# The block behind a rarely taken branch, laid ahead of the branch's arm instead of behind it

## The chip, the cores and the metric

The kernel runs on one core of one Trainium2 chip. The metric is the device time of one execution in microseconds (us). The core has five engines, each with an instruction sequence of its own: PE (matrix products), DVE and ACT (vector and scalar work), POOL (here above all the issue of transfers) and SP (transfers). They wait for each other through semaphores.

## What is computed

Attention within a band of 32 positions to each side, in 8 batches of 8 heads with 576 positions of 64 values, followed by a mixture of 8 experts of which each token takes one:

```python
def _attn_ref(q, k, v):
    scores = scale * np.matmul(q, k.transpose(0, 1, 3, 2))
    mask = np.abs(pos[:, None] - pos[None, :]) <= window
    scores = np.where(mask, scores, -1000000000.0)
    ...
    return np.matmul(attn, v).astype(np.float32)

def _moe_ref(x, modality_id, w_gate, modality_bias, w1, w2):
    logits = x @ w_gate + modality_bias[modality_id]
    e_idx = np.argmax(logits, axis=1)
    ...
    for e in range(E):
        mask = e_idx == e
        h = np.maximum(x[mask] @ w1[e], 0.0)
        out[mask] = gate_w[mask, None] * (h @ w2[e])
```

There are 4608 tokens of 512 values; `w1` is 512 x 1024 and `w2` 1024 x 512 for each expert.

## The kernel before, in words

The program has two ways to the result. The **main part** is a fast way that rests on assumptions about the data: that only one expert is in use for each of the two modalities, that the sorted tokens of one modality fill about half of the list, that the sums of the softmax are in a normal range. It is written out by hand: the string `ORDER` lists its steps, and a loop calls the function of each step in that order, so every engine gets its instructions in the order of the string. Each batch's heads go through scores (`SA`, `SB`), exponentials (`sa`, `sb`), the band's mask (`M`), the product with the values (`V`) and the division by the sums (`v`). `X` sorts a block's tokens by modality, `pa` and `pb` append them to the two ends of `XT`. The expert's two products follow in tiles of 256 tokens (`U` at line 916, `u` at 931 and 933, `D` at 942), `y` scales the rows (952 and 954), and `O` (961) writes them to their places in the output with a scatter that POOL issues. Tile 18, the last, is a small one for the tokens where the two modalities meet.

The steps `c0` to `c16` check the assumptions along the way and count what breaks them; `c17` (line 1028) loads that count, `Ct["flag"]`, into a register of each of the five engines. In `ORDER` `c17` stands between the last scaling and the last two scatters:

```
... D18.0.0:2 y17.0/v O17.1/p D18.0.1 y18.0/a c17 O17.0/p O18.0/p
```

The **general arm**, `general()`, is a slow way that holds for any data. It stands under `tc.If(Ct["flag"] > 0, ...)` at line 1211 and computes everything anew, in loops over heads, batches and experts. With the inputs that are timed the count is zero, and the arm doesn't run.

The branch is compiled into three blocks for each engine besides the main part. The *arm* is `general()` with its loops. The *block behind the branch* is what runs in the arm's place: each engine waits for its own work and counts its semaphores up to where the arm would leave them. On POOL that is a row of waits for the eight software queues, thus for all scatters, and one instruction that adds to their semaphores (ISA in the order, INC_SWDGE_SEM in the profile). The profile gives this block line 1211, like the branch itself. The *end block* (line 1239) follows in both cases: SP checks all semaphores, the engines meet in a barrier, which POOL collects, POOL clears the semaphores, and they meet once more.

Before the change, these blocks lie in memory as main part, arm, block behind the branch, end block. The main part ends with a compare-and-branch on every engine. With a count above zero it falls through into the arm; with zero it jumps over the arm to the block behind the branch, which runs on into the end block.

Of the kernel before, what the change touches and what calls it, by code (L numbers as in the profile page):

```python
# [94 lines left out]
def kernel(  # L95
# [98 lines left out]
    Ct = {}  # L194
# [1013 lines left out]
            nc.sync.dma_start(ov[bass.ds(i, 1)].rearrange("a (t p) d -> p (a t) d", p=TB), acc)  # L1208

    tail = const.tile([P, 1], FP32)  # L1210
    with tc.If(Ct["flag"] > 0, preferred_fallthrough_block=True):
        for _ in range(1):
            nc.gpsimd.memset(tail[:], 0.0)
        general()
# [29 lines left out]
```

## Time and profile before

| | |
|---|---|
| time, median of 3 runs | 209.22 us (208.91 to 209.65) |
| the profiled execution's own time | 209.1 us |
| its span, first to last instruction | 207.5 us |
| granted TensorE clock, mean | 0.996 |
| PE, matrix products | 194.9 us busy, 94% of the span |
| DVE | 149.9 us, 72% |
| ACT | 133.0 us, 64% |
| POOL | 98.9 us, 48% |
| fetches of instructions, queues q8 and q14 | 22 packets of 0.36 MB, 12 packets of 0.10 MB |

How to read the rows: engines' names are as above; PEld is PE's loading of weights, and a q behind a name (POOLq) marks an instruction of the engine's sequencer, which waits, branches or drains while the engine itself may be idle or busy with earlier work. Such instructions are not in the busy times. L1211 is line 1211 of the kernel. Starts are in us from the start of the span.

### The profile page before, as it was taken

How to read it: one execution, taken by the hardware profiler on the slowest of the kernel's cores; microseconds unless marked ns; L12 is line 12 of the kernel's file. 1: busy time of each engine (PE TensorE's matmuls, PEld its weight loads, DVE VectorE, ACT ScalarE, POOL GpSimd, SP SyncE). 2: the span in 40 equal slices, each digit the busy share in tenths (PEclk: the TensorE clock that was granted, in tenths of full speed). 3: DMA queues.
4: the chain of work that ended last, by engine and by line, in shares of the span. 5: the costliest groups of instructions: out<-in, count | busy, mean ns of one | idle time of the engine just before them, and what ended most of it. 6: DMA issues, size and time to landing. Idle time of an engine off the chain costs nothing. (4 is left out here: it accounts for less than half of the span.)

```text
span 207.5 us, 6240 instructions
## 1 busy us (share of the span) xinstructions
PE 194.9 (94%) x2585; PEld 139.8 (67%) x2585; DVE 149.9 (72%) x293; ACT 133.0 (64%) x226; POOL 98.9 (48%) x143
## 2 busy tenths in 40 slices
PE   7689789999999999999999999999999999999980
PEld 5568569867766588559766885687578669765630
DVE  3888999999899788779799988975378442803210
ACT  3484697669794987776588878579653547060620
POOL 7987695686051979288102830660321011331351
PEclk9999999999999999999999999999999999999998
DMA  4999999999999999989992890239121831221141
GB/s 67 202 174 185 211 209 193 212 193 212 200 186 234 169 211 213 206 115 206 186 171 68 97 175 0 83 128 113 51 102 53 332 128 54 103 101 51 54 158 57
DMA packets 47629, 30.41 MB, mean 147 GB/s; under 512 B 38851, under 2 KB 38891, under 8 KB 47339
## 3 DMA queue, kind: packets, MB, share of 16 engines
q0 software_dynamic: 46576, 27.79, 84.2%
q1 hardware_dynamic: 1019, 2.16, 3.0%
q8 instruction: 22, 0.36, 0.7%
q14 instruction: 12, 0.10, 0.1%
HBM read 36.76 MB, written 9.70 MB: 224 GB/s over the span
## 5 line engine op out<-in xcount | busy, mean ns | idle before, releaser
L961 POOL DMA_INDIRECT out_dram<-ys,ids x37 | 40.6, 1098 | 87.2 <-ACT ys L952 33.8
L916 PE MATMUL banks<-XT,w_sb 128*128 128x256 bf16 x576 | 71.4, 273 | 0.3 <-DVE xt L758 0.3
L942 PE MATMUL banks<-w_sb,hT 128*128 128x512 bf16 x288 | 69.8, 379 | 0.0
L916 PEld LDWEIGHTS <-w_sb 128*128 128x128 bf16 x576 | 53.8, 98 | 10.9 <-issue 1.3
L695 ACT ACTIVATE pt<-banks 128x1536 bf16<-128x1536 f32 x32 | 46.4, 1453 | 14.0 <-PE banks L687 9.5
L933 ACT ACTIVATE hT<-banks 128x512 bf16<-128x512 f32 x57 | 33.0, 600 | 30.0 <-PE banks L916 27.5
L942 PEld LDWEIGHTS <-hT 128*128 128x128 bf16 x296 | 26.7, 98 | 25.6 <-issue 0.6
L655 DVE STREAM_TRANSPOSE qk<-qk 128x576 int32<-128x576 int32 x32 | 38.5, 1244 | 1.8 <-DMA qk<-in_q_dram 1.1
L712 DVE TENSOR_TENSOR pt<-pt,mask 128x1920 bf16<-128x1920 bf16 x28 | 32.1, 1169 | 3.5 <-ACT pt L695 3.4
L758 DVE TENSOR_TENSOR xt<-banks,recs 128x640 bf16<-128x640 f32 x32 | 26.4, 824 | 1.2
L729 PEld LDWEIGHTS <-pt 128*128 128x128 bf16 x576 | 21.2, 97 | 3.6 <-issue 0.4
L729 PE MATMUL banks<-vt,pt 128*128 128x65 bf16 x576 | 22.7, 193 | 0.4 <-DVE pt L712 0.2
L931 DVE TENSOR_SCALAR hT<-banks 128x512 bf16<-128x512 f32 x17 | 11.5, 685 | 15.9 <-PE banks L916 15.9
L952 ACT ACTIVATE ys<-banks,Gt 128x512 f32<-128x512 f32 x20 | 13.7, 691 | 12.9 <-PE banks L942 12.1
L798 ACT CAST XT<-banks 128x352 f32 (+3 forms) x40 | 18.0, 449 | 5.7 <-PE banks L778 4.9
L687 PE MATMUL banks<-qk 32*128 32x192 bf16 (+1 forms) x640 | 18.8, 239 | 2.5 <-DVE oh_ab L613 1.6
L231 POOL DMA_DIRECT2D vt<-in_v_dram x16 | 20.5, 1285 | 0.2 <-issue 0.2
L954 DVE TENSOR_SCALAR ys<-banks,Gt 128x512 f32<-128x512 f32 x17 | 12.7, 744 | 10.3 <-PE banks L942 4.7
L812 ACT CAST XT<-banks 128x352 f32 (+2 forms) x39 | 17.6, 452 | 1.9 <-PE banks L778 1.3
L687 PEld LDWEIGHTS <-qk 32*128 32x128 bf16 x640 | 12.3, 93 | 9.6 <-issue 6.8
L970 PE MATMUL banks<-zero_b 128*128 128x256 bf16 x88 | 13.1, 297 | 1.8 <-POOL zero_b L320 1.3
L778 PEld LDWEIGHTS <-xt 128*128 128x128 bf16 x160 | 10.5, 98 | 4.9 <-issue 0.8
(157 smaller groups left out, 146.3 us busy)
## 6 DMA issues: line engine op xcount, KB each, us to landing
vt<-in_v_dram POOLq DMA_DIRECT2D x16, 288.0 KB
w_sb<-in_moe_w_dram POOLq DMA_DIRECT2D x4, 1024.0 KB
qk<-in_q_dram POOLq DMA_DIRECT2D x7, 576.0 KB
qk<-in_k_dram POOLq DMA_DIRECT2D x7, 576.0 KB
wx<-w_sb SPq DMA_DIRECT2D x2, 1024.0 KB, 6.2
out_dram<-ys,ids POOLq DMA_INDIRECT x37
qk<-in_k_dram POOLq DMA_DIRECT2D x2, 288.0 KB
qk<-in_q_dram POOLq DMA_DIRECT2D x2, 288.0 KB
```

The costliest lines, as they stand in the source:

```text
L231: nc.gpsimd.dma_start(v_t[b % NV][:, n_ * i:n_ * i + n_, 0:D], v[b].rearrange("h s d -> (h s) d").rearrange("(n p) d -> p n d", p=P)[:, n_ ...
L655: nc.vector.transpose(qk_t[b % 2][:, g, at:at + S].rearrange("p (t r) -> p r t", r=R), Ct["l", b][:, u, g].bitcast(I32).rearrange("p (r j) ...
L687: nc.tensor.matmul(st[:, h, WIN * i_:WIN * i_ + w_], qk[32 * h:32 * h + 32, c_, QK + k0:QK + k0 + P], qk[32 * h:32 * h + 32, c_, q0:q0 + w ...
L695: nc.scalar.activation(pt[:, :, 2 * part:2 * part + 2, 0:WIN], st[:, :, 0:2 * WIN].rearrange("p h (j c) -> p h j c", c=WIN), ACT.Exp, scal ...
L712: nc.vector.tensor_tensor(out=p_ap, in0=p_ap, in1=mask[:], op=ALU.mult)
L729: nc.tensor.matmul(o_ap, pt[:, c1:c1 + P], vt[:, g0 + j, 0:D + 1], start=(m == 0 and i_ == 0), stop=(i_ == len(mine) - 1), skip_group_chec ...
L758: nc.vector.tensor_tensor(out=o_ap, in0=o_v[:, :, :, 0:D], in1=rec.unsqueeze(3).to_broadcast([P, 2, NM, D]), op=ALU.mult)
L798: ins = nc.scalar.copy(XT[:, :, bass.ds(r_, w_)], Ct["X", b, m][:, :, 0:w_])
L916: ins = nc.tensor.matmul(ph[:, u_, :], w1[:, f0:f0 + 2 * P - 1:2], rhs, start=(kd == 0), stop=(kd == n_kd - 1))
L933: nc.scalar.activation(o_ap, i_ap, ACT.Relu)
L942: nc.tensor.matmul(Ct["D", t_, s_], Ct["h", t_][:, kf, P * s_:P * s_ + P], w2, start=(kf == 0), stop=(kf == n_kf - 1))
L961: ins = nc.gpsimd.indirect_dma_start(out=out, out_offset=bass.IndirectOffsetOnAxis(ap=ids[:, u_:u_ + 1], axis=0), in_=Ct["y", t_, s_][:], ...
```

## The change

One argument of the branch is turned round:

```diff
-    with tc.If(Ct["flag"] > 0, preferred_fallthrough_block=True):
+    with tc.If(Ct["flag"] > 0, preferred_fallthrough_block=False):
         for _ in range(1):
             nc.gpsimd.memset(tail[:], 0.0)
         general()
```

After it the blocks lie as main part, block behind the branch, arm, end block. The compare-and-branch falls through into the block behind the branch when the count is zero, and jumps to the arm when it is not. At the end of the block behind the branch stands an unconditional branch over the arm to the end block. The instructions are the same in kind and number on every engine, and everything ahead of the compare-and-branch stands where it stood.

On POOL, at the end of the main part: the last scatters, the branch, and what follows it in memory (the queues' semaphores are DMASW0 to DMASW7; `tail` is the first tile that the arm writes).

```order
 L961 DMA out_dram<-ys,ids 4608x512 [waits DMASW2_49,Activation_49]
 L1211 COMPARE_AND_BRANCH
+L1211 ISA [waits Pool_49,DMASW4_49,DMASW5_49,DMASW3_49,DMASW6_49,DMASW2_49,DMASW7_49,DMASW1_49,DMASW0_49]
+L1211 UNCONDITIONAL_BRANCH
 L1213 MEMSET tail 128x1
 L1079 MEMSET XT 96x960 [waits PE_49]
```

The block behind the branch, with its waits for all eight queues, now follows the compare-and-branch. On POOL at the other end of the arm, whose last loop is at line 1154, and at the start of the end block (line 1239):

```order
 L1154 COMPARE_AND_BRANCH
 L1154 UNCONDITIONAL_BRANCH
-L1211 ISA
-L1211 UNCONDITIONAL_BRANCH
 L1239 ISA
```

There the two rows are gone, so that the arm runs on into the end block. Between the compare-and-branch and the old place of the block lie 58 rows on POOL, 59 on DVE, 21 on ACT and 40 on SP. On PE it is the same move, here at the end of the main part, behind the load of the count; the arm there has 422 rows, so that the jump over it is the longest:

```order
 L1028 TENSOR_LOAD fl_i
 L1211 COMPARE_AND_BRANCH
+L1211 UNCONDITIONAL_BRANCH
 L1095 COMPARE_AND_BRANCH
 L1095 UNCONDITIONAL_BRANCH x2
```

PE's wait for its own last product, which the order doesn't list as a row, stands between these two L1211 rows.

## The prediction

> **What bounds the kernel now.** I read the page first, then the chain of work that ended last, then the timeline of the last ten microseconds, then the rows of the two source lines at which the branch and the end of the program stand. The diff leaves everything ahead of the branch as it is, so only that tail can change.
>
> ```profile
> span 207.5 us, 6240 instructions
> ...
> 202.28 0.14 issue
> 202.43 0.97 POOL out_dram L961
> ```
>
> The first row is from the page, the other two are the whole chain of waits: it ends with a scatter of output rows that POOL issues at 202.43. The span ends at 207.5, so some 4 us stand behind the last instruction that the chain knows. The rows of the timeline show what finishes last on the other engines (start, duration, engine and line):
>
> ```profile
> 199.53 1.89 PE L942 MATMUL banks<-wx,hT 128*128 128x512 bf16 x8
> ...
> 201.46 0.69 ACT L952 ACTIVATE ys<-banks,Gt 128x512 f32<-128x512 f32 x1 [2.77 <-PE banks L942]
> 202.43 0.97 POOL L961 DMA_INDIRECT out_dram<-ys,ids  x1 [0.63 <-ACTq L1211]
> ```
>
> PE's last product is done at 201.4, ACT scales it until 202.15, POOL scatters it. What fills the rest are the sequencers' instructions (the q behind an engine's name), which the page doesn't count as busy. Line 1211 is the branch with the block that lies behind the arm; each row has the count, the shortest, median and longest duration in ns, and the first and last start:
>
> ```profile
> L1211 SPq EVENT_SEMAPHORE  x8: 3/16/17, 197.8 to 199.0; - x8
> L1211 POOLq EVENT_SEMAPHORE  x5: 17/42/2372, 202.7 to 205.4; - x5
> L1211 SPq COMPARE_BRANCH  x1: 45/45/45, 197.3 to 197.3; - x1
> L1211 PEldq COMPARE_BRANCH  x1: 3842/3842/3842, 198.0 to 198.0; - x1
> L1211 DVEq COMPARE_BRANCH  x1: 72/72/72, 200.5 to 200.5; - x1
> L1211 DVEq EVENT_SEMAPHORE  x1: 21/21/21, 201.0 to 201.0; - x1
> L1211 ACTq COMPARE_BRANCH  x1: 45/45/45, 201.8 to 201.8; - x1
> L1211 PEldq EVENT_SEMAPHORE  x1: 51/51/51, 202.0 to 202.0; - x1
> L1211 POOLq COMPARE_BRANCH  x1: 50/50/50, 202.2 to 202.2; - x1
> L1211 ACTq EVENT_SEMAPHORE  x1: 17/17/17, 202.3 to 202.3; - x1
> L1211 POOLq INC_SWDGE_SEM  x1: 376/376/376, 205.5 to 205.5; - x1
> ```
>
> The flag is zero, so every engine takes the branch past the arm. On SP, DVE, ACT and POOL the next instruction starts 0.5 us after the branch (197.3 to 197.8, 200.5 to 201.0, 201.8 to 202.3, 202.2 to 202.7). On PE the branch alone takes 3.84 us. POOL then waits for the scatters: one of its five waits lasts 2.37 us, and the last starts at 205.4. INC_SWDGE_SEM counts up the software queues' semaphores from 205.5 to 205.9. SP has been waiting for just that (engine, line, releaser; total, times, longest):
>
> ```profile
> SPq L1239 <- DMA out_dram<-ys,ids: 6.7, 1, 6.7
> ```
>
> The rows of line 1239, the block at the end, between 205.5 and 206.75:
>
> ```profile
> L1239 SPq EVENT_SEMAPHORE  x12: 28/28/28, 205.8 to 206.5; - x12
> L1239 SPq DRAIN  x2: 7/10/13, 206.5 to 206.6; - x2
> L1239 POOLq DRAIN  x1: 788/788/788, 205.9 to 205.9; - x1
> L1239 POOLq EVENT_SEMAPHORE  x1: 17/17/17, 206.7 to 206.7; - x1
> ```
>
> Two strands run side by side from 205.8. SP makes twelve checks and reports to the barrier at 206.6. POOL drains for 0.79 us, to 206.7, and then collects the reports. So the tail is: landing of the last scatter (205.4), counting up (205.9), POOL's drain or SP's checks (206.7 and 206.6), then barrier and reset to 207.5. The other three engines reported long before, in the same view between 200 and 203:
>
> ```profile
> L1239 DVEq DRAIN  x1: 17/17/17, 201.1 to 201.1; - x1
> L1239 PEldq DRAIN  x1: 8/8/8, 202.1 to 202.1; - x1
> L1239 ACTq DRAIN  x1: 8/8/8, 202.3 to 202.3; - x1
> ```
>
> **The change, part by part.** The instructions on the path that runs are the same. Before, the order was main part, jump, waits, end; now it is main part, waits, jump, end. One jump stays; it moves to the other side of the waits. A jump that stood ahead of a wait, and was hidden by it, stands behind it.
>
> *The first branch falls through.* Each engine saves its taken branch: 0.5 us on SP, DVE, ACT and POOL, 3.84 us on PE. Worth: nothing. On POOL those 0.5 us stand ahead of the wait of 2.37 us for the scatter. PE, DVE and ACT wait in the barrier from 202.3 at the latest until 206.7, SP until 205.8. Without that cover the saving would be 0.5 us.
>
> *The waits move ahead of the jump.* Their number and what they wait for don't change: 0. But PE's wait is for its own last product, so its jump can't start before 201.4, where the old one started at 198.0, with products still queued.
>
> *The jump to the end block.* The trace of before doesn't show this instruction away from its target: POOL's INC_SWDGE_SEM ends at 205.9 and its DRAIN starts at 205.9. So its cost is bounded below by 0, which excludes a gain, and above by the 3.84 us of PE's branch. I take for each engine what its own branch took, since start and target are, to within a few instructions, the same places: 0.5 us on four, 3.84 us on PE. The order shows why PE stands apart: over 400 rows are skipped there, 59 or fewer on the others.
>
> - PE: 201.4, the wait's 0.05, 3.84: 205.3. It is needed in the barrier at 206.6. Cover 1.3 us; cost 0.
> - SP: from 199.0, 0.5 us later; needed at 205.8. DVE and ACT report at 201.6 and 202.8 instead of 201.1 and 202.3. Cost 0.
> - POOL: this is the one with no wait behind it. INC_SWDGE_SEM ends at 205.9, so the DRAIN starts at 206.4, not 205.9. What follows hangs on what the 788 ns are.
>
> ```profile
> L966 POOLq DRAIN  x1: 4507/4507/4507, 177.4 to 177.4; - x1
> ...
> 178.19 0.97 POOL L961 DMA_INDIRECT out_dram<-ys,ids  x1 [0.30 <-DVE lo__146 L857]
> ...
> L1239 POOLq DRAIN  x2: 46/78/109, 206.9 to 207.2; - x2
> ```
>
> With nothing in flight a drain on POOL takes 46 to 109 ns (the two later ones). With a scatter queued ahead of it, it takes 4.5 us, until 181.9, some 2.7 us beyond the end that the trace gives the scatter. A drain is thus as long as what is in flight, and the 788 ns should be the rest of INC_SWDGE_SEM, which ends at 206.7 whenever the drain is issued. Then a drain issued at 206.4 still ends at 206.7: cost 0. If instead the 788 ns belong to the drain itself, it ends at 207.2: cost 0.5 us. Those are the two ends; I take 0, since the rows at 177.4 and 206.9 fit the first reading and 788 ns fits none of the idle ones.
>
> *Fetches of instructions.* They move too (bytes in MB and share of 16 DMA engines, from 202.4 to the end):
>
> ```profile
> q0 software_dynamic: 152, 0.24, 13.1%
> q8 instruction: 1, 0.02, 1.4%
> q14 instruction: 2, 0.02, 1.1%
> ```
>
> They hold the engines a fifth as long (2.5 against 13.1) as the data packets that POOL's wait is for. If all of that left the scatter's 2.4 us, it would gain, I estimate, at most 0.3 us; as PE's fetch now starts at 201.4, most stays. I take 0 and keep 0.3 us as the lower bound.
>
> The sum is 0 against the profiled execution's own 209.1 us (span 207.5 and 1.6 around it). That execution lies 0.1 below the median of 209.22, so the forecast in terms of the median is 209.2.
>
> [...]
>
> **The rivals.**
>
> *POOL's drain costs its 0.79 us wherever it stands.* Then the 0.5 us are paid in full: 209.1 + 0.5 = 209.6, or 209.7 in terms of the median (0.24% more). For it: the drain's end (206.7) and SP's report (206.6) lie so close that nothing else hides a late drain. Against it: the drains of 46 to 109 ns.
>
> *POOL's jump finds its target not loaded.* This is the slower side. What PE's branch cost then stands on POOL between 205.9 and the drain: 205.9 + 3.84 + 0.1 = 209.8 in place of 206.7, that is 3.1 us: 212.3. It decides from a jump longer than 0.8 us (206.7 less 205.9). Against it: POOL's branch of before went from the same place to within eight instructions of the same target in 0.05 us, with 0.5 to the next instruction. For it: the wait in between, and a target those few instructions further on. [...]
>
> *PE arrives late.* Its fetch would have to take more than 5.1 us (201.45 to 206.6) where it took 3.84. Every further microsecond would then be paid; with 6 us it is 0.9, so 210.1.
>
> *The saved branch counts.* If the first jump delayed what ends last, its 0.5 us would come off, with the 0.3 us of traffic at most: 209.2 less 0.8, so 208.4 (0.38% less). Against it is the 2.37 us wait behind POOL's jump.
>
> **How the numbers follow.** About 0.3% (0.63 us) is what a measurement of this kernel can tell from no change. Forecast (no change, 209.2): 0.68. Drain rival (209.7, within that bound): 0.18. POOL's fetch (212.3): 0.06. PE late (210.1): 0.03. A gain: 0.05, of which I give 0.03 to 208.4 and 0.02 to a smaller one within the bound. So faster 0.03, same 0.68 + 0.18 + 0.02 = 0.88, slower 0.06 + 0.03 = 0.09. The range takes in the forecast, the drain rival and the gain, with the scatter of the three runs of before (0.3 below their median, 0.4 above): from 208.9 less 0.3, so 208.6, to 209.7 with most of that scatter, so 210.0. POOL's fetch stays out.
>
> **What would show it.** Before the change PE's COMPARE_BRANCH at 198.0 lasts 3.84 us; after, it should be under 0.1, its EVENT_SEMAPHORE should end at 201.4, and its first DRAIN of line 1239 should come at 205.3 to 205.4, not 202.1. POOL's INC_SWDGE_SEM should end some 0.5 us ahead of its first DRAIN, and that DRAIN should last about 0.3 us; if it again lasts 0.79, the drain rival is right. SP's twelve checks should start with INC_SWDGE_SEM as before. The forecast is wrong if POOL's DRAIN starts microseconds behind INC_SWDGE_SEM, if PE's DRAIN comes after SP's at 206.6, or if anything ahead of 197 us moves.

## The result and the profile after

| | time, median | ratio to before, 95% interval |
|---|---|---|
| before, in the same runs | 209.73 us (9 runs) | |
| changed kernel | 211.07 us (9 runs, 210.36 to 212.59) | 1.0063 (1.0038 to 1.0088) |

The changed kernel is slower by 1.3 us, 0.6%: beyond the range that was given. That range goes by a median of 209.22 for the kernel before; 0.63% more than that is 210.5, beyond its upper end of 210.0 too. Part of the 1.3 us goes with the clock: three of the nine runs had a granted clock of 0.981 and took 211.7 to 212.6 us, the other six, at 0.988 to 0.993, took 210.4 to 211.3. The profiled execution took 210.36 us. First the two branches of line 1211 and the block between them, in the view of that line (count; shortest, median and longest ns; first and last start). The profile calls both COMPARE_BRANCH, though the second is the unconditional one:

```profile
span 208.8 us, 6245 instructions
...
L1211 POOLq EVENT_SEMAPHORE  x5: 17/43/3456, 202.4 to 206.1; - x5
...
L1211 PEldq COMPARE_BRANCH  x2: 95/2102/4110, 198.1 to 201.7; - x2
...
L1211 POOLq COMPARE_BRANCH  x2: 38/41/44, 202.3 to 206.6; - x2
...
L1211 PEldq EVENT_SEMAPHORE  x1: 51/51/51, 201.5 to 201.5; - x1
...
L1211 POOLq INC_SWDGE_SEM  x1: 376/376/376, 206.2 to 206.2; - x1
```

The move is there: PE's first branch takes 95 ns, the second starts at 201.7, behind the last product, and takes 4.11 us. POOL's wait for the scatters lasts 3.46 us from 202.6, and INC_SWDGE_SEM starts at 206.2 instead of 205.5. Then the end block, in the view of line 1239 from 202 to 208.1:

```profile
L1239 SPq EVENT_SEMAPHORE  x12: 27/28/28, 206.5 to 207.2; - x12
L1239 SPq DRAIN  x2: 7/10/13, 207.3 to 207.4; - x2
L1239 POOLq EVENT_SEMAPHORE  x2: 17/17/17, 208.0 to 208.1; - x2
L1239 ACTq DRAIN  x1: 80/80/80, 202.8 to 202.8; - x1
L1239 PEldq DRAIN  x1: 73/73/73, 205.9 to 205.9; - x1
L1239 POOLq DRAIN  x1: 840/840/840, 207.1 to 207.1; - x1
```

POOL's drain starts at 207.1, 0.5 us behind INC_SWDGE_SEM's end at 206.6, and lasts 840 ns, 52 more than before. SP reports at 207.4 and waits for POOL, which checks at 208.0. PE reports at 205.9, in time.

So the tail grew in two places. From the start of INC_SWDGE_SEM to POOL's check it took 1.25 us before (205.45 to 206.70) and takes 1.78 now (206.20 to 207.98): **0.53 us**. And the last scatter, issued at 202.50 against 202.43, landed at 206.03 against 205.29: **0.7 us** in this pair of profiles. Together they make 1.3 us of span (207.5 to 208.8); the last product ended at 201.50 against 201.42, so the main part gave nothing.

The landing needs a look at the DMA packets. For 202.4 to 204.6 the view of the queues says:

```profile
q0 software_dynamic: 151, 0.25, 31.3%
q8 instruction: 1, 0.02, 4.9%
q14 instruction: 1, 0.01, 1.0%
```

The one packet of q8 is 16 KB of instructions; 4.9% of 16 engines over 2.2 us is 1.73 us on one engine. Packets carry neither an address nor an engine's name in the trace: that this one is PE's, with the jump's target in it, is read from the time at which it comes. In the list of packets it runs from 202.70 to 204.43, from 1.01 us behind the start of PE's long branch (201.69) to 1.37 ahead of its end (205.80). Before, a q8 packet from 199.00 to 200.47 has the same place in PE's branch (197.99 to 201.83): 1.01 behind its start, 1.36 ahead of its end. In the changed kernel the last four 4 KB packets of the scatter start only at the packet's end, at 204.42 to 205.24. Of the scatter's 16 semaphore updates, 15 are in by 204.70; the sixteenth comes at 206.03. The profile of before has a packet beside its last scatter too (202.65 to 203.78): it starts 0.82 us behind the end of PE's branch, so by the same reading it holds what stands behind the target. In both kernels a fetch of PE's stands before the last piece of the last scatter.

The chain of waits shows nothing of either. It ends at the same scatter, since the last 5 us are all sequencer:

```profile
202.37 0.09 issue
202.46 0.02 POOLq L1211
202.48 0.02 issue
202.50 0.97 POOL out_dram L961
```

### The profile page after: what moved, and what is told of

Same layout as the page of the kernel before. It is cut to its first block, busy times and chain, and to the rows that moved or that the text cites. A ratio compares the mean times of both kernels' runs of the same rounds, so it can differ in the third digit from the quotient of the medians.

```text
span 208.8 us, 6245 instructions
## 1 busy us (share of the span) xinstructions
PE 195.4 (94%) x2585; PEld 140.1 (67%) x2585; DVE 149.4 (72%) x293; ACT 133.1 (64%) x226; POOL 99.3 (48%) x143
## 5 line engine op out<-in xcount | busy, mean ns | idle before, releaser
L970 PE MATMUL banks<-zero_b 128*128 128x256 bf16 x88 | 13.8, 308 | 1.8 <-POOL zero_b L320 1.3
```

## The experiments

Theory A: POOL's jump now stands behind its last wait, and its drain has a length of its own. Theory B: PE's fetch of instructions lies in the way of the last scatter. Rival C: the late landing was chance.

**The two kernels again, for profiles.** No edit.

> The changed kernel once more. In its first profile INC_SWDGE_SEM started 0.74 us later than in the one of before, because the last scatter landed later, and from there to POOL's barrier check it took 1.78 us in place of 1.25. Theory A (moved jump, and a drain with a length of its own): the 1.78 us come again, within 0.05. Theory B (PE's fetch of its jump target lies in the way of the last scatter): the wait for the scatter again ends at 206.0 or later, and one packet of the instruction queue of 16 KB takes over 1.5 us between 202 and 205. Rival C (the late landing was chance): the wait ends at 205.3 to 205.5 and the span is 208.1. Ratio to before 1.005 to 1.008 by A and B together, 1.0025 by A alone.

> The kernel before, once more, for a second profile. A: 1.25 us from the start of INC_SWDGE_SEM to POOL's barrier check. B: wait for the scatter ends at 205.3, span 207.5; C: it ends anywhere between 204.6 and 206.1, span 206.9 to 208.3.

> The kernel before, a third profile. Theory B: the second packet of PE's instructions ends 2.3 to 2.8 us behind PE's last product and the last scatter lands 1.0 to 1.6 us behind that end (landing 3.9 to 4.4 behind the last product). Rival C (chance, not the packet): the landing bears no relation to the packet's end.

> The changed kernel, a third profile. Theory B: the packet of the jump's target ends 2.6 to 3.4 us behind the last product, landing 1.0 to 1.6 us behind that end (4.0 to 4.9 behind the last product); theory A: 1.78 us from INC_SWDGE_SEM to the barrier check. Rival C: landing without relation to the packet.

The changed kernel's ratio was 1.0036 (1.0012 to 1.0059), medians 210.73 and 209.81; the three single runs took 209.82 and 211.36 us (before) and 212.60 (changed). The table is worked out from the traces' packets and semaphore updates; times in us, and "landing" is that of the last scatter.

| profile | PE's last product ends | end of q8 packet, after that | landing, after the packet's end | landing, after the last product | INC_SWDGE_SEM to check |
|---|---|---|---|---|---|
| before | 201.42 | 2.36 | 1.51 | 3.87 | 1.25 |
| before_again | 201.65 | 2.74 | 1.63 | 4.37 | 1.25 |
| before_third | 203.41 | 2.44 | 1.61 | 4.06 | 1.25 |
| after | 201.50 | 2.93 | 1.60 | 4.53 | 1.78 |
| after_again | 202.17 | 3.31 | 1.61 | 4.92 | 1.78 |
| after_third | 203.45 | 3.12 | 1.62 | 4.74 | 1.78 |

A's 0.53 us came back each time. The packet's end moves by a microsecond and the landing follows at 1.5 to 1.6 us. In all six, four 4 KB packets of the scatter run one behind the other, and the first starts within 0.03 us of the packet's end. C falls for the landing. On average it is at 4.10 before and 4.73 after: 0.63 us. With A's 0.53 that makes 1.16 us, 0.55% of 209.7, between the two measured ratios.

Three things came otherwise than expected. In before_again POOL's wait ended at 206.05 instead of 205.3, a time inside the range that was given for chance; by the table the packet's end moved with it (2.74 instead of 2.36). In after_again the packet took 1.06 us, not over 1.5. And the second ratio lies below the 1.005 to 1.008 of A and B together, while its interval takes in the 1.0025 of A alone. So these times don't show B by themselves; the packets do, and the next experiments. Chance has its part elsewhere: the main part, which is the same program, ended its last product anywhere from 201.4 to 203.5.

**A short arm, in both layouts.** The general arm is left out; POOL gets eight small transfers in its place, so that the block behind the branch stays as it was there.

```diff
             nc.gpsimd.memset(tail[:], 0.0)
-        general()
+        for i in range(8):
+            nc.gpsimd.dma_start(lo_[:, i, 0:1], tail[:])
```

> Leaves the general arm out and puts one memset and eight small transfers of POOL in its place, so no arm stands on PE and PE needs no far jump and no new page of instructions; block behind the branch still behind the arm, as before. B: no 16 KB packet of instructions after 200 us, the last scatter lands at 204.7 in place of 205.3, time 0.6 us below before (ratio 0.997). If fetches don't matter: ratio 1.000, landing 205.3. A says nothing here but that INC_SWDGE_SEM to barrier check stays 1.25 us.

> The same short arm, with the block behind the branch ahead of the arm. POOL still jumps behind INC_SWDGE_SEM, now over 11 instructions. A: DRAIN starts 0.5 us behind INC_SWDGE_SEM's end and lasts 0.8: 0.5 us more than the short arm with the block behind (ratio between them 1.0025), landing the same 204.7. If the drain had only been late because of something of the long arm, the two short ones agree within 0.1 us. B: both short ones lack the late landing, so this one stands at before less 0.1 us, over 1 us below the changed kernel.

Block behind the arm: 208.94 us, ratio 0.9959 (0.9933 to 0.9985). Block ahead: 208.91 us, 0.9956 (0.9925 to 0.9987). The queues from 198 to 207 of the second have no instructions at all (the other is alike):

```profile
q0 software_dynamic: 400, 1.05, 31.0%
```

Both landed 3.20 us behind the last product, 0.9 us ahead of the average of before. That is what B expects. A's size was missed: the two are within 0.1 us of each other, and POOL's rows of the short arm with the block ahead say why (1240 is the end block here):

```profile
L1211 POOLq COMPARE_BRANCH  x2: 38/41/44, 202.4 to 205.4; - x2
L1211 POOLq INC_SWDGE_SEM  x1: 376/376/376, 205.0 to 205.0; - x1
...
L1240 POOLq DRAIN  x3: 46/103/791, 205.6 to 207.0; - x3
```

A jump over 11 instructions starts at 205.45 and the drain follows at 205.62: 0.18 us, not the 0.48 us of the jump over the whole arm. From INC_SWDGE_SEM to the check it takes 1.42 us with the block ahead and 1.25 with the block behind, a difference that the times are too coarse to show. The drain lasted 791 ns, as in the other layout, so its length doesn't depend on when it starts, even here.

**PE's arm within reach.** 90 of the 112 products of the experts are left out of the arm, each of them two instructions, so that PE jumps over 308 instructions instead of 488 (the expectation says 96, which is miscounted: 48 of 64 and 42 of 48 go). The other engines' jumps stay.

```diff
-                        for kd in range(n_kd):
-                            nc.tensor.matmul(hp, w1_sb[:, 0, kd, P * kf:P * kf + P], xT[:, kd, hs], ...)
+                        nc.tensor.matmul(hp, w1_sb[:, 0, 0, P * kf:P * kf + P], xT[:, 0, hs], ...)
...
-                    for kf in range(n_kf):
-                        nc.tensor.matmul(dp, hT[:, kf, ...], w2_sb[:, 0, kf], ...)
+                    nc.tensor.matmul(dp, hT[:, 0, ...], w2_sb[:, 0, 0], ...)
```

> The kernel before with 96 of the 112 products of the experts left out of the general arm (which doesn't run), so that PE's jump spans 308 instructions in place of 488; the other engines' jumps stay within a few instructions of what they were. In four profiles so far the last scatter landed 1.5 to 1.6 us behind the end of a 16 KB packet of PE's instructions, 3.9 to 4.9 us behind PE's last product; without a packet it landed at 3.2. Theory B: PE's branch takes 0.05 to 0.5 us in place of 3.5 to 3.8, the packet behind it runs near 199 to 200.5, ahead of the last scatter, which then lands 3.2 us behind the last product: 0.7 to 1.2 us below before (ratio 0.995). Rival: the stall itself, or the branch's distance on the other engines, sets the time: ratio 1.000 to 0.999.

> The changed kernel with the same 96 products left out of the arm. PE's jump starts behind its last product and doesn't stall, but the page behind its target is fetched from there. Theory B: a 16 KB packet between 202.3 and 204.5 still lies in the way, landing 3.9 to 4.9 us behind the last product; with A's 0.53 us it is as slow as the changed kernel (ratio to before 1.003 to 1.006), though PE reports to the barrier 4 us earlier. Rival (PE's stall is what counts): 0.5 us slower than the one with the block behind, ratio to before 0.998.

With the block behind the arm: 208.65 us, ratio 0.9965 (0.9939 to 0.9992). PE's branch takes 358 ns, a q8 packet comes at 198.89 to 200.10, and the scatter lands at 3.23. With the block ahead: 210.09 us, 1.0046 (1.0021 to 1.0071), between the changed kernel's two ratios. Its rows (1207 is the branch, 1235 the end block):

```profile
L1207 PEldq COMPARE_BRANCH  x2: 95/202/310, 197.8 to 201.5; - x2
L1207 POOLq COMPARE_BRANCH  x2: 38/41/44, 202.1 to 205.8; - x2
...
L1235 SPq DRAIN  x2: 7/10/13, 206.5 to 206.6; - x2
L1235 PEldq DRAIN  x1: 72/72/72, 201.8 to 201.8; - x1
L1235 POOLq DRAIN  x1: 841/841/841, 206.3 to 206.3; - x1
```

PE doesn't stall (310 ns) and reports at 201.8, four microseconds earlier than in the changed kernel, and the ratio shows no gain from that. Here a q8 packet comes at 202.73 to 204.01, and the scatter lands at 3.95, 0.7 us later than with the block behind. So PE's stall of 4.11 us costs nothing by itself here; the time at which the packet comes does. The profile is of the fastest of the ten runs, and in it the scatter lands earlier than in any profile of the changed kernel, as late as in those of before: how long the packet lies in the way varies.

**The flag later.** The kernel before, with one step of the order moved, so that PE branches 2 us later.

```diff
-... u17.2/a c15/v c16/a D17.1.1 O14.0/p D17.0.0:6 D17.0.1 y17.1/a D18.0.0:2 ...
+... u17.2/a c15/v D17.1.1 O14.0/p D17.0.0:6 D17.0.1 y17.1/a c16/a D18.0.0:2 ...
```

> The kernel before with one step of the order moved: ACT casts the count (c16) behind its scaling y17.1 instead of ahead of it, so that the flag comes some 2 us later and PE branches at 200.0 instead of 198.0. Theory B: the two packets of PE's instructions move to about 201 to 202.4 and 204.6 to 205.7; the first ends ahead of the last scatter's turn and the second starts behind it, landing 3.2 to 3.5 us behind the last product, 0.4 to 0.9 us below before (ratio 0.996 to 0.998), and PE's report at 204 is still in time for 206. Rival (a fetch anywhere in the last 5 us costs the same): ratio 1.000. If the second packet starts ahead of 203.9 it collides worse: ratio 1.002.

208.86 us, ratio 0.998 (0.995 to 1.001): unclear. The runs fall into two groups, seven at 208.3 to 209.0 and five at 209.9 to 210.5. The profile is of the second: the packet came at 204.11, not behind the scatter but into it (the expectation had put the collision at starts ahead of 203.9), ended at 205.59, and the scatter landed at 206.64, 4.89 behind the last product and 1.05 behind the packet. That the first group are the runs in which the packet missed the scatter fits B, but none of that group was profiled.

**A drain ahead of the branch.** The changed kernel with a drain of POOL behind the last scatter.

```diff
-y18.0/a c17 O17.0/p O18.0/p
+y18.0/a c17 O17.0/p O18.0/p N/p
```

> The changed kernel with a drain of POOL added as the last instruction of the main part, behind the last scatter, in the shadow of its landing. The end block's drain lasted 788 to 840 ns in six profiles, wherever it started. Theory A1 (the first drain behind scatters has this length of its own, and a drained engine has little left): the end block's drain lasts about 0.1 us, POOL is ready behind SP, and the tail from INC_SWDGE_SEM to the barrier check is 1.2 in place of 1.78 us. Theory A2 (INC_SWDGE_SEM brings it): it lasts 0.84 again, the tail stays 1.78. Both expect the added drain to end ahead of the landing; if it ends later than that, the time rises.

210.54 us, ratio 1.0052 (1.0023 to 1.0081). The added drain (966), the rest of POOL and SP's report:

```profile
L966 POOLq DRAIN  x1: 3518/3518/3518, 202.0 to 202.0; - x1
...
L1211 POOLq INC_SWDGE_SEM  x1: 185/185/185, 206.0 to 206.0; - x1
...
L1239 SPq DRAIN  x2: 7/10/13, 207.0 to 207.0; - x2
...
L1239 POOLq DRAIN  x1: 108/108/108, 206.8 to 206.8; - x1
L1239 POOLq EVENT_SEMAPHORE  x1: 17/17/17, 207.1 to 207.1; - x1
```

The end block's drain falls from 840 to 108 ns, as A1 expects: INC_SWDGE_SEM alone doesn't bring the length, it goes with the first drain behind the scatters. POOL is ready ahead of SP's report: 1.01 us from INC_SWDGE_SEM to the check (206.05 to 207.06), 0.77 less than in the changed kernel. But the added drain ends at 205.5, not ahead of the landing at 205.09 as both theories expected. From the landing to INC_SWDGE_SEM it now takes 0.96 us instead of 0.17, so what the end saves was paid ahead of it.

This profile, of the fastest of the ten runs, shows something else. PE's program is that of the changed kernel, and the packet still runs from 202.43 to 203.70, with four 4 KB packets of the scatter from its end on; but it ends 2.48 us behind the last product, and the scatter lands at 3.87, as early as in before. So the changed layout brings PE's packet into the scatter's way each time, but it doesn't always end later there than the second packet of before.

**A hint for PE's branch.** The kernel before, whole, with one instruction more on PE.

```diff
+    op["H"] = lambda _: tc.mark_branch_hint_location("arm", "LikelyTaken", [ET.PE])
...
-    with tc.If(Ct["flag"] > 0, preferred_fallthrough_block=True):
+    with tc.If(Ct["flag"] > 0, preferred_fallthrough_block=True, label="arm"):
```

with the step `H` added to the order; in the program it stands at PE's start (BRANCH_PREFETCH_HINT, 50 ns at 1.0 us).

> The kernel before, whole, with a hint instruction on PE at the start of its program that tells the sequencer that the branch at the end is likely taken (the branch gets a label for it). Theory B: if the hint makes PE load the target page ahead, PE's branch takes 0.05 to 0.5 us, the packet behind it runs at 199 to 200.5, and the last scatter lands 3.2 us behind PE's last product: ratio 0.995 to 0.998, the same as with the short PE arm. If the hint has no effect so far from its branch: branch 3.5 to 3.8 us, landing 3.9 to 4.4, ratio 1.000.

208.97 us against 209.56, ratio 0.9968 (0.9939 to 0.9997): faster than the kernel before by 0.3%, with an interval that ends just below 1, and with the general arm unchanged. The branch is at line 1212 and the end block at 1240:

```profile
L1212 PEldq COMPARE_BRANCH  x1: 398/398/398, 198.1 to 198.1; - x1
...
L1212 POOLq INC_SWDGE_SEM  x1: 376/376/376, 204.9 to 204.9; - x1
...
L1240 SPq DRAIN  x2: 7/10/13, 205.9 to 206.0; - x2
...
L1240 POOLq DRAIN  x1: 788/788/788, 205.3 to 205.3; - x1
```

The queues from 202.4 to 206.5, with no row for q8:

```profile
q0 software_dynamic: 160, 0.26, 17.6%
q14 instruction: 2, 0.02, 1.2%
```

PE's branch takes 0.40 us instead of 3.84. A q8 packet comes at 199.31 to 200.40, ahead of the last scatter, which lands 3.20 us behind the last product. There are 21 packets on q8 instead of 22. The two packets of the other instruction queue, q14, run beside the last scatter here too (203.28 to 203.88) and don't make it late, so it is q8's packet that does. The hint on top of the changed layout, which would leave A alone, was not tried.

## Why the prediction was wrong

*What bounds the kernel* was read rightly: the landing of the last scatter, INC_SWDGE_SEM, POOL's drain beside SP's checks, the barrier. Ahead of the branch no cost of the change shows: the last product ended at 201.4 to 203.4 in the three profiles of before and at 201.5 to 203.5 in those of the changed kernel.

*The first branch falls through, worth nothing*: right. The branches of 95 ns on PE and 44 ns on POOL brought no time.

*PE: 205.3, cover 1.3 us, cost 0*: right for the barrier (205.9, needed at 207.4), and the short PE arm, with a branch of 310 ns and no gain, showed that the stall costs nothing by itself. The rival that PE arrives late did not happen in any profile.

*The jump on POOL takes 0.5 us*: right (0.48), and no profile shows the stall of the rival whose target isn't loaded.

*"The 788 ns should be the rest of INC_SWDGE_SEM, which ends at 206.7 whenever the drain is issued"*: **the first step that failed**. Issued 0.5 us later, the drain lasted 840 ns instead of 0.3. The rival that was priced at 0.5 us with a chance of 0.18 is what happened, at 0.53. The reading went by the long drain at line 966, where there was work in flight; a drain of 788 ns that starts behind a wait for the scatters' landing had a length of its own, which an earlier drain took away (108 ns).

*"Fetches of instructions: I take 0 and keep 0.3 us as the lower bound"*: **the second step that failed**, and the larger one, with 0.63 us on average of three profiles each. The packets were weighed by their share of sixteen engines, and the 0.3 us is given without its working. What the traces show is one late piece: 15 of the scatter's 16 semaphore updates were in by 204.70, and the sixteenth, behind the packet, at 206.03; POOL's wait ended at 206.06. The text saw that "PE's fetch now starts at 201.4", but looked only for what might leave the scatter's time, not for what might come in. By the times of the packets, the jump's target was fetched from 199.0 before, while PE still had products queued, and only the following packet met the scatter (202.65 to 203.78). Behind the wait for PE's own last product the target's packet meets it, and ends 0.6 us later behind that product (3.12 against 2.51 on average of the table).

The distance by which the prediction set PE apart shows in the variants: PE's branch took 3.4 to 4.5 us where it jumped over 488 instructions without a hint, 0.3 to 0.4 over 308 or with a hint. The unconditional branches of the changed kernel took 38 to 51 ns on POOL, DVE and ACT; POOL's next instruction came 0.48 us behind the start of its own.

## What to carry to other kernels

Here a jump was free ahead of a wait and cost 0.5 us behind the last one: in choosing a layout, look at what each engine still has to wait for on either side of it. With PE's far jump a fetch of instructions moved too, and the landing with it, by 0.63 us on average: such a packet belongs in the plan of the transfers. Look when it runs and which transfer's last piece stands behind it. Where a far branch has a usual way, try a hint early in the program; here it took 0.3% off.

## What the runs showed of the hardware that was not expected

- A 16 KB packet of PE's instructions held back the last piece of the scatter that ran beside it: in six profiles of the two kernels the landing came 1.5 to 1.6 us behind the packet's end, in three variants 1.05 to 1.39 behind it. Without a packet beside it, it came 3.20 to 3.23 us behind the last product (four profiles), with one at 3.87 to 4.92 (nine). That the scatter's next 4 KB packet starts where the packet ends speaks for one DMA engine, but it was not seen directly; the packets in the trace carry the queue, not the engine.
- Behind a taken branch on POOL the next instruction came after 0.48 to 0.51 us over the long arm, and after 0.18 us over 11 instructions. Why was not tried.
- With all scatters landed, POOL's first drain behind them took 788 to 841 ns whenever it started, and 108 ns where a drain had gone before; INC_SWDGE_SEM then took 185 ns instead of 376.
- A hint at the start of PE's program took effect 197 us later: 0.40 us instead of 3.84 for the branch, with one fetch less.
